# A fallback path behind a flag: its transfers move from SyncE to GpSimd, and its DMA transposes become TensorE transposes

## The chip, the cores and the metric

The kernel runs on one core of one Trainium2 chip. A core has five engines with an instruction stream each: TensorE (in the profile PE for matmuls and PEld for weight loads), VectorE (DVE), ScalarE (ACT), GpSimd (POOL) and SyncE (SP). SP does no arithmetic; it issues transfers. A "q" behind an engine's name (SPq, POOLq) means its sequencer: register, branch, semaphore and transfer-issuing instructions. The metric is device time in microseconds. The time before is 358.01 us, the median of three runs (357.88 to 358.39).

## What is computed

Causal attention with a decay that depends on the input, followed by a normalisation and a gated feed-forward layer. Batch 8, 8 heads, 576 positions, head size 64; 4608 tokens of width 512, feed-forward width 1536:

```
scores = q k^T / 8 + min(cum[j] - cum[i], 0),  cum = cumsum(max(s, 0)),  causal
x   = softmax(scores) v            # heads side by side: 4608 x 512
xn  = x / rms(x) * g
out = (silu(xn w_gate) * (xn w_val)) w_out
```

Inputs and output are float32.

## The kernel before

The program has two ways to the result. The fast path, which is nearly all of the code, folds the decay into a factor on the keys and computes exponentials without subtracting a row maximum. That holds only while scores and decay sums stay in a certain range. While it runs, it gathers what decides that: the largest absolute values of q and k (check_mag, check_max), the decay sums (decay_range) and the sums of squares. Near the end verdict() turns these into one integer, `flag_i`, on line 1063: 1 when the fast path's result stands.

The fast path walks the 4608 tokens in nine chunks of 512. For each chunk, ffn(c) (line 936) goes through 12 blocks of 128 feed-forward columns, with four matmuls for the gate (line 946) and four for the value (line 955) each, then through four blocks of 128 tokens with 12 matmuls into the output (line 972). The order of the rest is written by hand: between the matmul groups, step() puts in the attention of later tokens, by due times in slots. The whole fast path stands under one manual schedule, so its order on every engine is that of the code. At the end of each block of tokens, ACT copies the result out of PSUM (line 976) and SP stores it (line 977). The last block is stored in two parts of 384 and 128 columns. SP also issues the fast path's DMA transposes (lines 190 and 495) and some of its loads; GpSimd issues most loads.

After the fast path, general() (line 1261) is called. Line 1269 loads the flag into a register of each engine, and line 1270 opens a block that runs only when the flag is 0. When the flag is 1, each engine branches over the block:

```
flag = nc.values_load(flag_i[0:1, 0:1], min_val=0, max_val=1)
with tc.If(flag == 0, preferred_fallthrough_block=True):
```

The block computes the same result with no assumption on the range. It spills the decay sums to DRAM and has two loops. The first (line 1283) runs over the 64 pairs of batch and head: it loads q, k and v, transposes q and k on TensorE, and for each of five blocks of queries computes the scores, an ordinary softmax and the product with v; the result goes to a scratch tensor in DRAM (`x_d`). The second (line 1366) runs over the 72 groups of 64 tokens: it reads the eight heads back, normalises, transposes the 64 x 512 block, runs the feed-forward layer in three groups of 512 columns with a transpose each, and stores. Each loop ends its turn with a barrier of all engines.

Semaphores carry all order between engines. The compiler gives each transfer one of eight semaphores for those issued by SP and ACT, or one of eight for those issued by GpSimd, and each engine has its own. They count up through the program, and an instruction waits for a count. So where the block is jumped over, each engine runs a few semaphore instructions behind the branch that bring the counts to where the block would have left them; in the profile these have the line of the block, 1270. At the end of the program (line 1432, the launch), SP waits for all semaphores in twelve instructions of two each; then the engines meet in barriers and GpSimd clears the semaphores.

In the compiled program SP has 274 instructions up to its branch over the block, 186 in the block, 8 semaphore instructions for the jumped-over block, and 17 at the end.

Of the kernel before, what the change touches and what calls it, by code (L numbers as in the profile page):

```python
# [9 lines left out]
BF16 = mybir.dt.bfloat16  # L10
# [16 lines left out]
def kernel(  # L27
# [1228 lines left out]
    fast.close()  # L1256

    general(ctx, tc, q, k, v, out, wg_sb, wv_sb, wout_sb, g_row, cum, ident_bf, flag_i)


def general(ctx, tc, q, k, v, out, wg_sb, wv_sb, wout_sb, g_row, cum, ident_bf, flag_i):
    nc = tc.nc
    B, H, S, D = q.shape
    DM, FB, CC, NSC, BH = H * D, 12, 4, 5, B * H

    def rows(c):
        return 128 if c < 4 else 64

    flag = nc.values_load(flag_i[0:1, 0:1], min_val=0, max_val=1)
    with tc.If(flag == 0, preferred_fallthrough_block=True):  # L1270
        with tc.tile_pool(name="gd", bufs=1, space=bass.MemoryType.DRAM) as gd, \
             tc.tile_pool(name="gs", bufs=1) as gs, \
             tc.tile_pool(name="gp", bufs=1, space=bass.MemoryType.PSUM) as gp:
            cum_d = gd.tile([BH, S], FP32, name="cum_d")
            x_d = gd.tile([9 * BH + 56, 64, D], FP32, name="x_d")
            half = gs.tile([128, 1], FP32, name="half")
            nc.vector.memset(half, -0.5)
            nc.sync.dma_start(out=cum_d, in_=cum)
            qf = q.rearrange("b h s d -> (b h) s d")
            kf = k.rearrange("b h s d -> (b h) s d")  # L1280
            vf = v.rearrange("b h s d -> (b h) s d")
# [1 line left out]
            with tc.For_i(0, BH, 1) as i:  # L1283
                one = bass.ds(i, 1)
                nat = gs.tile([128, 2, NSC, D], BF16, name="nat")
                vn = gs.tile([128, NSC, D + 1], BF16, name="vn")
                crow = gs.tile([128, S], FP32, name="crow")
                ccol = gs.tile([128, NSC], FP32, name="ccol")
                nc.vector.memset(nat, 0.0)
                nc.vector.memset(vn, 0.0)  # L1290
                nc.vector.memset(vn[:, :, D:D + 1], 1.0)
                nc.vector.memset(ccol, 0.0)
                for w, src in ((0, kf), (1, qf)):
                    nc.gpsimd.dma_start(out=nat[:, w, 0:4, :], in_=src[one, 0:512, :].rearrange(
                        "o (c p) d -> p (o c) d", p=128))
                    nc.gpsimd.dma_start(out=nat[0:64, w, 4, :], in_=src[one, 512:576, :].rearrange(
                        "o p d -> p (o d)"))
                nc.gpsimd.dma_start(out=vn[:, 0:4, 0:D], in_=vf[one, 0:512, :].rearrange(
                    "o (c p) d -> p (o c) d", p=128))
                nc.gpsimd.dma_start(out=vn[0:64, 4, 0:D], in_=vf[one, 512:576, :].rearrange(  # L1300
                    "o p d -> p (o d)"))
                nc.sync.dma_start(out=crow, in_=cum_d[one, :].to_broadcast([128, S]))
                nc.sync.dma_start(out=ccol[:, 0:4], in_=cum_d[one, 0:512].rearrange(
                    "o (c p) -> p (o c)", p=128))
                nc.sync.dma_start(out=ccol[0:64, 4:5], in_=cum_d[one, 512:576].rearrange(
                    "o p -> p o"))
                kqt = gs.tile([D, 2, 640], BF16, name="kqt")
                for w in (0, 1):
                    pt = gp.tile([D, 640], BF16, name="pt")
                    for c in range(NSC):  # L1310
                        nc.tensor.matmul(pt[:, c * 128:(c + 1) * 128], lhsT=nat[:, w, c, :],
                                         rhs=ident_bf, is_transpose=True,
                                         start=(c == 0), stop=(c == NSC - 1))
                    nc.vector.tensor_copy(out=kqt[:, w, :], in_=pt)
                for qb in range(NSC):
                    n = rows(qb)
                    nk = qb * 128 + n
                    sp = gp.tile([128, 1024], FP32, name="sp")
                    nc.tensor.matmul(sp[0:n, 0:min(nk, 512)], lhsT=kqt[:, 1, qb * 128:qb * 128 + n],
                                     rhs=kqt[:, 0, 0:min(nk, 512)], start=True, stop=True)  # L1320
                    if nk > 512:
                        nc.tensor.matmul(sp[0:n, 512:nk], lhsT=kqt[:, 1, qb * 128:qb * 128 + n],
                                         rhs=kqt[:, 0, 512:nk], start=True, stop=True)
                    sc = gs.tile([128, 640], FP32, name="sc")
                    nc.vector.tensor_scalar(out=sc[0:n, 0:nk], in0=crow[0:n, 0:nk],
                                            scalar1=ccol[0:n, qb:qb + 1], scalar2=0.0,
                                            op0=ALU.subtract, op1=ALU.min)
                    nc.vector.scalar_tensor_tensor(out=sc[0:n, 0:nk], in0=sp[0:n, 0:nk],
                                                   scalar=0.125, in1=sc[0:n, 0:nk],
                                                   op0=ALU.mult, op1=ALU.add)  # L1330
                    nc.gpsimd.affine_select(out=sc[0:n, qb * 128:nk], in_=sc[0:n, qb * 128:nk],
                                            pattern=[[-1, n]], compare_op=ALU.is_ge,
                                            fill=-1.0e30, base=0, channel_multiplier=1)
                    mx = gs.tile([128, 1], FP32, name="mx")
                    nc.vector.tensor_reduce(out=mx[0:n], in_=sc[0:n, 0:nk], axis=AX.X, op=ALU.max,
                                            negate=True)
                    pr = gs.tile([128, 640], BF16, name="pr")
                    nc.vector.memset(pr, 0.0)
                    nc.scalar.activation(out=pr[0:n, 0:nk], in_=sc[0:n, 0:nk], func=AF.Exp,
                                         bias=mx[0:n])  # L1340
                    pq = gp.tile([128, NSC, 128], BF16, name="pq")
                    for c in range(qb + 1):
                        nc.tensor.matmul(pq[:, c, :], lhsT=pr[:, c * 128:(c + 1) * 128],
                                         rhs=ident_bf, is_transpose=True,
                                         start=(c == 0), stop=(c == qb))
                    prT = gs.tile([128, NSC, 128], BF16, name="prT")
                    nc.vector.tensor_copy(out=prT[:, 0:qb + 1, :], in_=pq[:, 0:qb + 1, :])
                    av = gp.tile([128, D + 1], FP32, name="av")
                    for c in range(qb + 1):
                        nc.tensor.matmul(av, lhsT=prT[:, c, :], rhs=vn[:, c, :],  # L1350
                                         start=(c == 0), stop=(c == qb))
                    rz = gs.tile([128, 1], FP32, name="rz")
                    nc.vector.reciprocal(out=rz[0:n], in_=av[0:n, D:D + 1])
                    xo = gs.tile([128, D], FP32, name="xo")
                    nc.vector.tensor_scalar(out=xo[0:n], in0=av[0:n, 0:D], scalar1=rz[0:n],
                                            scalar2=None, op0=ALU.mult)


                    for j in range(2 * qb, min(2 * qb + 2, 9)):
                        m = j * 64 - qb * 128  # L1360
                        nc.sync.dma_start(
                            out=x_d[bass.ds(i * 9 + 8 * j, 1)].rearrange("o p d -> p (o d)"),
                            in_=xo[m:m + 64])

            ov = out.rearrange("(t p) d -> t p d", p=64)
            with tc.For_i(0, B * 9, 1) as t:
                xb = gs.tile([64, H, D], FP32, name="xb")
                for h in range(H):
                    nc.sync.dma_start(
                        out=xb[:, h, :],  # L1370
                        in_=x_d[bass.ds(t * 8 + 9 * h, 1)].rearrange("o p d -> p (o d)"))
                sq = gs.tile([64, H, D], FP32, name="sq")
# [5 lines left out]
                xs = gs.tile([64, DM], BF16, name="xs")  # L1378
# [1 line left out]
                                               scalar=ssg, in1=g_row[0:64], op0=ALU.mult,  # L1380
                                               op1=ALU.mult)
                xT = gs.tile([128, CC, 64], BF16, name="xT")
                nc.sync.dma_start_transpose(out=xT, in_=xs)
                Hg = gs.tile([64, 3, DM], BF16, name="Hg")
                HT = gs.tile([128, 3, CC, 64], BF16, name="HT")
                for fc in range(3):
                    fs = slice(fc * DM, (fc + 1) * DM)
                    gv = gp.tile([64, 2, DM], FP32, name="gv")
                    for j, w in ((0, wg_sb), (1, wv_sb)):
                        for cc in range(CC):  # L1390
                            nc.tensor.matmul(gv[:, j, :], lhsT=xT[:, cc, :], rhs=w[:, cc, fs],
                                             start=(cc == 0), stop=(cc == CC - 1))
# [3 lines left out]
                    nc.vector.scalar_tensor_tensor(out=ug, in0=tg, scalar=1.0, in1=gv[:, 0, :],  # L1396
                                                   op0=ALU.add, op1=ALU.mult)
                    nc.vector.tensor_tensor(out=Hg[:, fc, :], in0=ug, in1=gv[:, 1, :], op=ALU.mult)
                    nc.sync.dma_start_transpose(out=HT[:, fc], in_=Hg[:, fc, :])
                og = gp.tile([64, DM], FP32, name="og")  # L1400
                for fb in range(FB):
                    nc.tensor.matmul(og, lhsT=HT[:, fb // CC, fb % CC, :], rhs=wout_sb[:, fb, :],
                                     start=(fb == 0), stop=(fb == FB - 1))
                ob = gs.tile([64, DM], FP32, name="ob")
                nc.scalar.activation(out=ob, in_=og, func=AF.Copy, scale=0.5)
                nc.sync.dma_start(out=ov[bass.ds(t, 1)].rearrange("o p d -> p (o d)"), in_=ob)


# [28 lines left out]
```

## Time and profile before

| what | value |
|---|---|
| median of three runs | 358.01 us |
| the profiled execution, in all | 358.63 us |
| its span, first to last instruction | 357.0 us |
| granted TensorE clock over the span | 0.997 |
| flag written (line 1063) | at 336.2 us |
| last matmul ends, by the chain of work | about 350.8 us |
| last instruction | 357.0 us |

The first page of the profile gives the busy time of each engine, the queues and the chain of work that ended last. Semaphore, branch and transfer-issuing instructions are not counted as busy there; they are seen by asking for one line of the kernel, which lists its instructions with count, shortest, median and longest duration in ns, and the start of the first and the last. A window limits such a list to a stretch of time, so two windows show on which side of a moment instructions lie. A row of a DMA queue gives packets, megabytes and the share of 16 engines in the window. The queues named "instruction" (q8 and q14) load the engines' code.

### The profile page before, as it was taken

How to read it: one execution, taken by the hardware profiler on the slowest of the kernel's cores; microseconds unless marked ns; L12 is line 12 of the kernel's file. 1: busy time of each engine (PE TensorE's matmuls, PEld its weight loads, DVE VectorE, ACT ScalarE, POOL GpSimd, SP SyncE). 2: the span in 40 equal slices, each digit the busy share in tenths (PEclk: the TensorE clock that was granted, in tenths of full speed). 3: DMA queues.
4: the chain of work that ended last, by engine and by line, in shares of the span. 5: the costliest groups of instructions: out<-in, count | busy, mean ns of one | idle time of the engine just before them, and what ended most of it. 6: DMA issues, size and time to landing. Idle time of an engine off the chain costs nothing.

```text
span 357.0 us, 6944 instructions
## 1 busy us (share of the span) xinstructions
PE 344.7 (97%) x2419; PEld 165.5 (46%) x2419; DVE 276.6 (77%) x524; ACT 213.4 (60%) x471; POOL 204.8 (57%) x337
## 2 busy tenths in 40 slices
PE   5989999999999999999999999999999999999993
PEld 2454444544444444544444544445444454444441
DVE  6587989598967887898889887988798579818820
ACT  3988785878786546864676467654665454223321
POOL 7968754457669977677697987597545400000000
PEclk9999999999999999999999999999999999999998
DMA  7999999999969999999899999495410221020011
GB/s 231 136 196 265 179 176 265 179 204 186 95 126 173 158 165 115 240 131 208 150 165 102 115 158 147 48 133 102 112 22 17 73 76 23 0 106 13 1 62 63
DMA packets 130528, 45.68 MB, mean 128 GB/s; under 512 B 110548, under 2 KB 125656, under 8 KB 130488
## 3 DMA queue, kind: packets, MB, share of 16 engines
q0 software_dynamic: 67056, 13.70, 49.8%
q1 hardware_dynamic: 53936, 24.26, 33.0%
q10 hardware_dynamic: 9496, 7.23, 8.2%
q8 instruction: 20, 0.33, 0.4%
q14 instruction: 20, 0.16, 0.2%
HBM read 37.90 MB, written 9.44 MB: 133 GB/s over the span
## 4 chain that ended last, share of the span: by engine, by line
PE 87%; POOL 3%; DVE 3%; issue 2%; ACT 1%; DMA 1%; SPq 0%; POOLq 0%; DVEq 0%
PE psF L972 26%; PE psF L955 23%; PE psF L946 23%; PE psS L286 2%; PE psAV L443 2%; PE psAV L437 2%; PE psF L367 2%; PE psS L367 1%; DMA kqT<-kqn 1%; POOL v_sb L409 1%; DVE x_sb L453 1%; PE psAV L1118 1%; DVE Ht L951 1%; DVE U L958 1%; PE psS L255 1%
## 5 line engine op out<-in xcount | busy, mean ns | idle before, releaser
L946 PE MATMUL psF<-xnT,wg_sb 128*128 128x512 bf16 x432 | 110.9, 379 | 0.3 <-ACT xnT L511 0.3
L955 PE MATMUL psF<-xnT,wv_sb 128*128 128x512 bf16 x432 | 111.0, 379 | 0.0
L949 ACT ACTIVATE T<-psF 128x512 f32<-128x512 f32 x108 | 64.6, 598 | 63.0 <-PE psF L946 60.9
L972 PE MATMUL psF<-wout_sb,Ht 128*128 128x512 bf16 (+2 forms) x444 | 100.9, 374 | 0.0
L958 DVE SCALAR_TENSOR_TENSOR U<-T,psF 128x512 bf16<-128x512 f32 x108 | 73.6, 682 | 24.1 <-ACT T L949 23.9
L951 DVE TENSOR_TENSOR Ht<-U,psF 128x512 bf16<-128x512 bf16 x99 | 67.8, 685 | 6.9
L972 PEld LDWEIGHTS <-Ht 128*128 128x128 bf16 x444 | 40.1, 98 | 43.5 <-issue 1.4
L955 PEld LDWEIGHTS <-wv_sb 128*128 128x128 bf16 x432 | 39.6, 98 | 44.5 <-issue 2.9
L946 PEld LDWEIGHTS <-wg_sb 128*128 128x128 bf16 x432 | 39.4, 98 | 42.9 <-issue 2.4
L976 ACT ACTIVATE osb<-psF 128x512 f32<-128x512 f32 (+2 forms) x37 | 21.7, 586 | 58.2 <-PE psF L972 51.6
L384 POOL TENSOR_SCALAR_AFFINE_SELECT E<-E 128x512 bf16<-128x512 bf16 (+1 forms) x50 | 34.8, 704 | 28.3 <-ACT E L380 18.5
L194 POOL DMA_DIRECT2D v_sb<-in_v_dram x40 | 35.2, 882 | 0.2 <-issue 0.2
L484 DVE SCALAR_TENSOR_TENSOR xs_sb<-x_sb,al_all,g_row 128x512 bf16<-128x512 bf16 (+1 forms) x36 | 29.6, 822 | 4.1 <-POOL al_all L477 3.9
L474 POOL TENSOR_SCALAR al_all<-ss_all 128x1 f32<-128x1 f32 (+2 forms) x39 | 11.5, 295 | 37.0 <-ACT xs_sb L461 29.0
L310 ACT ACTIVATE E<-psS,biasK 128x256 bf16<-128x256 f32 (+3 forms) x88 | 29.1, 425 | 2.6 <-PE psS L286 2.6
L453 DVE TENSOR_TENSOR x_sb<-psAV,rZ 128x256 bf16<-128x256 f32 (+1 forms) x66 | 28.0, 424 | 2.3
L522 DVE TENSOR_TENSOR acc<-acc,mag 128x1280 bf16<-128x1280 bf16 x32 | 27.3, 872 | 0.2
L477 POOL TENSOR_TENSOR al_all<-al_all,mhalf 128x1 f32<-128x1 f32 (+2 forms) x39 | 25.1, 645 | 3.2
L443 PEld LDWEIGHTS <-E 128*128 128x128 bf16 x320 | 21.7, 98 | 10.5 <-POOL E L384 0.7
L461 ACT ACTIVATE xs_sb<-x_sb 128x512 bf16<-128x512 bf16 (+1 forms) x37 | 23.3, 629 | 4.6 <-DVE x_sb L453 4.0
L409 POOL TENSOR_TENSOR v_sb<-v_sb,vwx 128x512 bf16<-128x512 bf16 x25 | 25.9, 1037 | 0.1
L443 PE MATMUL psAV<-v_sb,E 128*128 128x65 bf16 x264 | 23.8, 194 | 0.1
(136 smaller groups left out, 381.8 us busy)
## 6 DMA issues: line engine op xcount, KB each, us to landing
out_dram<-osb SPq DMA_DIRECT2D x35, 256.0 KB, 2.4
kq<-in_q_dram ACTq DMA_DIRECT2D x5, 1024.0 KB, 7.2
v_sb<-in_v_dram POOLq DMA_DIRECT2D x32, 128.0 KB, 5.1
kqn<-in_k_dram POOLq DMA_DIRECT2D x20, 128.0 KB, 4.8
kq<-in_k_dram SPq DMA_DIRECT2D x4, 512.0 KB, 6.0
kq<-in_q_dram SPq DMA_DIRECT2D x4, 512.0 KB, 7.6
wout_sb<-in_moe_w_out_dram POOLq DMA_DIRECT2D x2, 768.0 KB, 10.2
kq<-in_q_dram POOLq DMA_DIRECT2D x1, 1024.0 KB, 10.5
```

The source lines that it names most:

```text
L194: nc.gpsimd.dma_start(out=v_sb[0:n, b % 2, c, :, 0:64], in_=v[b, :, c * 128:c * 128 + n, :].rearrange("h p d -> p h d"))
L384: nc.gpsimd.affine_select(out=Ev, in_=Ev, pattern=[[0, 4], [1, nq]], compare_op=ALU.is_ge, fill=0.0, base=0, channel_multiplier=-1)
L409: nc.gpsimd.tensor_tensor(out=v_sb[:, b % 2, c, :, 0:64], in0=v_sb[:, b % 2, c, :, 0:64], in1=vwx[:, c, i:i + H].unsqueeze(2).to_broadcast ...
L443: nc.tensor.matmul(o, lhsT=d, rhs=v_sb[:, p, qb, h, :], start=(j == 0 and qb == 0), stop=(j == 3))
L453: nc.vector.tensor_tensor(out=xo[:, g * 256:(g + 1) * 256].rearrange("p (h d) -> p h d", h=4), in0=pv[R, :, 0:64], in1=rZ[R].unsqueeze(2). ...
L484: nc.vector.scalar_tensor_tensor(out=xs_sb[R, (b * NSC + qb) % NX, :], in0=x_sb[R, (b * NSC + qb) % NX, :], scalar=al_all[R, col:col + 1], ...
L946: nc.tensor.matmul(Gp, lhsT=wg_sb[:, cc, fs], rhs=xnT[:, cc, x0:x0 + DM], start=(cc == 0), stop=(cc == CC - 1))
L949: nc.scalar.activation(out=T, in_=Gp, func=AF.Tanh, scale=0.5)
L951: nc.vector.tensor_tensor(out=Ht[:, fb - 1, :], in0=pend[0], in1=pend[1], op=ALU.mult)
L955: nc.tensor.matmul(Vp, lhsT=wv_sb[:, cc, fs], rhs=xnT[:, cc, x0:x0 + DM], start=(cc == 0), stop=(cc == CC - 1))
L958: nc.vector.scalar_tensor_tensor(out=U, in0=T, scalar=1.0, in1=Gp, op0=ALU.add, op1=ALU.mult)
L972: nc.tensor.matmul(Op[:, p0:p1], lhsT=Ht[:, fb, tb * 128:(tb + 1) * 128], rhs=wout_sb[:, fb, p0:p1], start=(fb == 0), stop=(fb == FB - 1))
```

## The change

All edits lie in general(). Every transfer that SP issued there is issued by GpSimd: the spill of the decay sums, three loads in the first loop and its nine stores of results, the eight loads and the store of the second loop. The four DMA transposes of the second loop, which SP issued, become TensorE transposes: a helper turn() makes four 64 x 128 transposes into PSUM against the identity and copies the result to SBUF on VectorE. After the change SP issues nothing in the block. The fast path is not edited.

```
-            nc.sync.dma_start(out=cum_d, in_=cum)
+            nc.gpsimd.dma_start(out=cum_d, in_=cum)
...
-                nc.sync.dma_start(out=crow, in_=cum_d[one, :].to_broadcast([128, S]))
-                nc.sync.dma_start(out=ccol[:, 0:4], in_=cum_d[one, 0:512].rearrange(
+                nc.gpsimd.dma_start(out=crow, in_=cum_d[one, :].to_broadcast([128, S]))
+                nc.gpsimd.dma_start(out=ccol[:, 0:4], in_=cum_d[one, 0:512].rearrange(
...
-                nc.sync.dma_start(out=ccol[0:64, 4:5], in_=cum_d[one, 512:576].rearrange(
+                nc.gpsimd.dma_start(out=ccol[0:64, 4:5], in_=cum_d[one, 512:576].rearrange(
...
-                        nc.sync.dma_start(
+                        nc.gpsimd.dma_start(
                             out=x_d[bass.ds(i * 9 + 8 * j, 1)].rearrange("o p d -> p (o d)"),
                             in_=xo[m:m + 64])
+
+            def turn(dst, src):
+                px = gp.tile([128, NSC, 128], BF16, name="pq")
+                for c in range(CC):
+                    nc.tensor.matmul(px[:, c, 0:64], lhsT=src[:, c * 128:(c + 1) * 128],
+                                     rhs=ident_bf[0:64, 0:64], is_transpose=True,
+                                     start=(c == 0), stop=(c == CC - 1))
+                nc.vector.tensor_copy(out=dst, in_=px[:, 0:CC, 0:64])
...
-                    nc.sync.dma_start(
+                    nc.gpsimd.dma_start(
                         out=xb[:, h, :],
...
-                nc.sync.dma_start_transpose(out=xT, in_=xs)
+                turn(xT, xs)
...
-                    nc.sync.dma_start_transpose(out=HT[:, fc], in_=Hg[:, fc, :])
+                    turn(HT[:, fc], Hg[:, fc, :])
...
-                nc.sync.dma_start(out=ov[bass.ds(t, 1)].rearrange("o p d -> p (o d)"), in_=ob)
+                nc.gpsimd.dma_start(out=ov[bass.ds(t, 1)].rearrange("o p d -> p (o d)"), in_=ob)
```

## Prediction

> **What bounds the kernel now.** I read the first page for the engines and the chain, then the time by stretches, then the last twenty microseconds instruction by instruction, because the first two say that nothing else can move.
>
> ```profile
> span 357.0 us, 6944 instructions
> PE 344.7 (97%) x2419; PEld 165.5 (46%) x2419; DVE 276.6 (77%) x524; ACT 213.4 (60%) x471; POOL 204.8 (57%) x337
> ...
> PE 87%; POOL 3%; DVE 3%; issue 2%; ACT 1%; DMA 1%; SPq 0%; POOLq 0%; DVEq 0%
> ```
>
> TensorE is busy 97% of the span and makes 87% of the chain that ended last. That is all fast path. The line of general() that starts its block is 1270 and the launch is line 1432; here are all instructions that the trace has for line 1270 on the engines other than SP:
>
> ```profile
> L1270 POOLq COMPARE_BRANCH  x1: 45/45/45, 336.9 to 336.9; - x1
> L1270 POOLq INC_SWDGE_SEM  x1: 451/451/451, 337.8 to 337.8; - x1
> L1270 DVEq COMPARE_BRANCH  x1: 72/72/72, 341.7 to 341.7; - x1
> L1270 DVEq EVENT_SEMAPHORE  x1: 21/21/21, 342.3 to 342.3; - x1
> L1270 PEldq COMPARE_BRANCH  x1: 364/364/364, 349.6 to 349.6; - x1
> L1270 PEldq EVENT_SEMAPHORE  x1: 51/51/51, 350.9 to 350.9; - x1
> L1270 ACTq COMPARE_BRANCH  x1: 54/54/54, 351.4 to 351.4; - x1
> L1270 ACTq EVENT_SEMAPHORE  x1: 17/17/17, 351.9 to 351.9; - x1
> ```
>
> Every engine branches once, about 0.5 us later runs a few semaphore instructions, and is done. No operation of general()'s body is there: the flag says that the fast path is valid, and the block is jumped over. So no transfer, transpose or matmul of the diff is executed. What the change can alter is what an engine does because the block exists: the jump, the code that lies in between, and the semaphore instructions after the jump, which give the semaphores the counts that the block would have left (I call them catch-up). This matters only where an engine is on the path, that is, behind the last matmul, which the chain has in its last pieces (start, duration):
>
> ```profile
> 340.44 10.40 PE psF L972 x60
> 350.84 0.02 issue
> 350.86 0.28 ACT osb L976
> ```
>
> ```profile
> core 0: us, PE busy (x) PEld busy (x) DVE busy (x) ACT busy (x) POOL busy (x), PEclk, DMA share, GB/s
> 300.00:340.00 40.00, 40.00 (x187) 18.09 (x186) 27.74 (x47) 12.72 (x23) 0.00 (x0) 1.00 0.08 28
> 340.00:352.30 12.30, 10.83 (x63) 5.43 (x60) 1.38 (x2) 2.77 (x6) 0.00 (x0) 1.00 0.23 83
> 352.30:357.00 4.70, 0.00 (x0) 0.00 (x0) 0.00 (x0) 0.00 (x0) 0.00 (x0) 0.76 0.07 21
> ```
>
> From 352.3 on no engine works for 4.7 us. What runs there is SP. First its last stores, then line 1270 in two windows, then the end of the program (line 1432):
>
> ```profile
> L977 SPq DMA_DIRECT2D out_dram<-osb x2: 332/718/1103, 350.8 to 351.2; - x2
> ...
> DMA to landing us min/median/max: 2.5/2.7/2.9
> ```
>
> ```profile
> L1270 SPq EVENT_SEMAPHORE  x3: 17/17/17, 352.9 to 353.1; - x3
> L1270 SPq COMPARE_BRANCH  x1: 58/58/58, 352.3 to 352.3; - x1
> ```
>
> ```profile
> L1270 SPq EVENT_SEMAPHORE  x5: 17/17/17, 355.0 to 355.3; - x5
> ```
>
> ```profile
> L1432 SPq EVENT_SEMAPHORE  x12: 28/28/28, 355.4 to 356.1; - x12
> ```
>
> ```profile
> L1432 SPq EVENT_SEMAPHORE  x14: 17/28/28, 355.4 to 357.0; - x14
> L1432 SPq DRAIN  x3: 7/7/13, 356.1 to 356.5; - x3
> ```
>
> SP has eight catch-up instructions, one for each semaphore of its transfers; every other engine but POOL has one. Three run by 353.1, then 1.9 us pass, and the other five run from 355.0. The stores cannot explain the gap: the last is issued at 351.2 and lands at most 2.9 us later, at 354.1, and the fourth catch-up instruction belongs to an older store. The transfers in the gap are these:
>
> ```profile
> ## 3 DMA queue, kind: packets, MB, share of 16 engines
> q14 instruction: 1, 0.01, 1.8%
> q1 hardware_dynamic: 12, 0.00, 0.9%
> ```
>
> One packet that loads instructions lies between 353.1 and 354.9, beside the last dozen packets of the store. I take the gap as an instruction fetch: SP's code runs out between its third and fourth catch-up instruction. The page gives the size of such pieces:
>
> ```profile
> q8 instruction: 20, 0.33, 0.4%
> q14 instruction: 20, 0.16, 0.2%
> ```
>
> On q14 a packet is 8 KB. An instruction has 64 bytes in the compiled program, so a piece holds 128. Counted in that program (branch labels left out), SP has 274 instructions ahead of its branch, 186 more up to the first catch-up instruction, and the fourth is number 463 from zero. Two further fetches fit SP: packets in the windows 120.4 to 120.7 and 240.1 to 240.25,
>
> ```profile
> q14 instruction: 1, 0.01, 16.8%
> ```
>
> ```profile
> q14 instruction: 1, 0.01, 21.9%
> ```
>
> when SP, by its order of instructions, is just past numbers 79 and 207. Adding 128 gives 335, then 463: exactly the gap. A piece begins at 463; the one from 335 was loaded ahead at 240, so the jump itself found its target; the one from 463 was asked for only at the jump (352.4), and was there 2.6 us later.
>
> [...]
>
> **The change, part by part.**
>
> *SP's transfers inside the block (22 issues and 4 transposes in the code, 12 and 13 per turn of the two loops and one ahead).* Executed: none, cost 0. As code they are 1 + 36 + 31 instructions with their address arithmetic, plus 19 waits in the loop bodies, 16 resets and 16 catch-ups on the loops' own exits. Without them the 186 instructions shrink to about 67 (186 - 68 - 19 - 32), so the end of SP's program begins near number 340, in a piece that was loaded at 240 us. No piece begins in the 17 instructions that follow. The gap of 1.9 us goes.
>
> *The eight catch-up instructions of SP.* With no transfer of SP in the block there is nothing to catch up: eight fewer. Five of them cost 0.4 us after the gap (355.0 to 355.4), three 0.2 us before it.
>
> *What is late next.* SP now reaches the twelve paired waits of line 1432 at 352.9 instead of 355.4. They run at 0.7 us for twelve, 0.06 each. They wait for all semaphores, the last store's among them. SP would be through them at 353.6, but that store lands at 351.2 + 2.9 = 354.1. In the order of the program its pair is the eleventh, which now runs at 356.0, 1.0 before the end at 357.0. So the new end is 354.1 + 1.0 = 355.1: a gain of 1.9 us, all of it at the end. Of the 2.5 us by which SP comes earlier, 0.6 turn into a wait for the store. Bounds: with that pair first in the order, eleven more follow the landing and the end is 355.7; if the landing is as quick as the quickest of these two stores, 2.5, the end is 354.7.
>
> *POOL gets the transfers.* Executed: none. Its code grows by some 70 instructions, enough to put the jump's target outside what is loaded; bound 0 to 2.6 us (SP's fetch). It branches at 336.9 and is needed again only when SP is through, 354.1 at the earliest: 17 us of cover. Perhaps one or two more catch-ups for its semaphores, 0.1 us each, under the same cover. What it costs without cover is 2.6 us.
>
> *PE gets 16 transposes with their weight loads, DVE four copies, in code alone.* PE branches at 349.6, DVE at 341.7. If PE's longer code made its jump miss, it would come at 350.0 + 2.6 = 352.6, still ahead of 354.1. Cost 0, covered by the last store's landing. ACT's code stays as it is.
>
> *The fast path.* Its stores, transposes and loads keep their engines and order, so I count nothing.
>
> Sum against the profiled execution: 357.0 - 1.9 = 355.1 span. That execution took 358.63 in all, 0.6 above the median of 358.01 of the three runs. I carry the difference over: 358.01 - 1.9 = 356.1.
>
> **The rivals.** (a) *Half the gain.* The gap is peculiar to the profiled execution, or SP keeps its eight catch-ups after all and only the code moves. Then either the 1.9 us were not there to win, or the eighth catch-up waits for the landing (354.1) and 12 x 0.06 + 1.0 come behind it: 355.9 against 355.1. I count a gain of 0.7: 357.3. For it: one profile only. Against: the packet in the gap and the count that meets it. [...]
> (b) *The gap is a landing.* If the 355.0 were a store's landing, the same wait would reappear at the eleventh pair: end 356.0, gain 1.0, time 357.0. Against: the issue-to-landing row ends at 354.1.
> (c) *No change: the gap moves along.* My count of the shortened code is wrong and a piece that is not loaded begins at the start of the end block: SP goes on at 352.4 + 2.6 = 355.0, then twelve pairs and 1.0 to the end, 356.6: gain 0.4, time 357.6, within what can be told apart. It needs over 170 of the 186 instructions to stay.
> (d) *Slower: ACT fetches twice.* ACT is the next to last to branch (351.4, done 351.5). One fetch would end at 354.1 and cost nothing. Were its target and its end in two pieces not loaded, it would come at 356.7, SP's last pair would wait for it, and the end is 356.7 + 0.9 = 357.6, time 358.6. It decides from the point where ACT comes later than 356.1, where SP's last pair stands now. For it: ACT has little cover. Against: its code gets no instruction.
>
> **How the numbers follow.** Clean gain 70%, (a) 11%, (b) 6%, (c) 8%, (d) 5%. The three runs lie between 357.88 and 358.39, so 0.2% (0.7 us) is about what can be told from no change. Clean, (b) and half of (a) are faster: 82%; the other half and (c) are the same: 13%; slower 5%. The clean case alone gives 355.6 to 356.7 by the bounds above; the range for 8 in 10 takes in (b) and (a): 355.6 to 357.4.
>
> **What would show it.** In the changed profile: the same trace up to 352.3; on line 1270 no catch-up of SP and more on POOL near 337; the pairs of line 1432 starting near 352.9 with a wait of half a microsecond before the eleventh or so; the end near 355.1. Wrong if SP still has a gap with a fetch in it after its branch, if another engine's semaphore instruction on line 1270 or 1432 comes later than 354, if the last matmul ends elsewhere than 350.8, or if the time does not move though the gap is gone.

## The result and the profile after

The changed kernel takes 356.32 us (median of six runs, 356.02 to 357.16), against 358.39 us for the kernel before (six runs). The ratio is 0.9947, with a 95% interval of 0.9933 to 0.9961: 1.9 us less by the ratio, 2.1 us by the two medians. The profiled execution took 356.21 us, with a span of 354.7 us.

As before, nothing of general()'s body is in the trace. These are its instructions on line 1270, all engines, by the view of one line (count; shortest, median and longest duration in ns; first and last start):

```profile
L1270 POOLq EVENT_SEMAPHORE  x5: 17/43/43, 339.3 to 339.6; - x5
L1270 POOLq COMPARE_BRANCH  x1: 45/45/45, 336.6 to 336.6; - x1
...
L1270 DVEq COMPARE_BRANCH  x1: 72/72/72, 341.4 to 341.4; - x1
L1270 DVEq EVENT_SEMAPHORE  x1: 21/21/21, 342.0 to 342.0; - x1
...
L1270 PEldq EVENT_SEMAPHORE  x1: 51/51/51, 350.6 to 350.6; - x1
L1270 ACTq COMPARE_BRANCH  x1: 54/54/54, 351.1 to 351.1; - x1
L1270 ACTq EVENT_SEMAPHORE  x1: 17/17/17, 351.6 to 351.6; - x1
L1270 SPq COMPARE_BRANCH  x1: 58/58/58, 352.2 to 352.2; - x1
```

SP has its branch there and no catch-up. POOL has one semaphore instruction more than before, and its first comes 2.6 us behind its branch instead of 0.5. In the kernel before they are these, behind a branch at 336.9:

```profile
L1270 POOLq EVENT_SEMAPHORE  x4: 17/30/43, 337.4 to 337.7; - x4
```

The end of the program is now line 1440; SP's pairs there (its waits for two semaphores each), in two windows, then all of SP's instructions on that line, and what SP waited for:

```profile
L1440 SPq EVENT_SEMAPHORE  x10: 28/28/28, 352.7 to 353.3; - x10
```

```profile
L1440 SPq EVENT_SEMAPHORE  x2: 28/28/28, 353.7 to 353.7; - x2
```

```profile
L1440 SPq EVENT_SEMAPHORE  x14: 17/28/28, 352.7 to 354.6; - x14
L1440 SPq DRAIN  x3: 7/7/13, 353.8 to 354.1; - x3
```

```profile
SPq L1440 <- PEq L1440: 0.7, 2, 0.5
SPq L1440 <- DMA out_dram<-osb: 0.3, 1, 0.3
```

Ten pairs run at once from 352.7, half a microsecond behind the branch. The eleventh waits 0.3 us for the last store, and the program ends 1.0 us later. Before, the eleventh pair ran at 356.0.

The packet that the prediction saw in the gap is still there. In the changed kernel the queue q14 has from 352.4 to 354.0:

```profile
q14 instruction: 2, 0.02, 3.1%
```

The second of the two starts at 353.28, 1.1 us behind the start of SP's branch; the one in the gap before started at 353.42, also 1.1 us behind SP's branch (352.34). By this distance both are taken to be SP's. Now the pairs run on without waiting for it. So a packet in a gap does not by itself show that SP waited for the packet; the experiments below had to show that.

The chain of work ends the same way in both, a little earlier here (start, duration):

```profile
350.54 0.02 issue
350.56 0.28 ACT osb L976
```

So the span of 354.7 against 357.0 has two parts. Behind the start of the last copy (line 976) the end takes 4.15 us instead of 6.18, which is 2.0 us. The other 0.3 us lie ahead of it (350.56 against 350.86). The experiments below give no ground to put this second part down to the change: in their profiled executions the last copy starts anywhere from 349.9 to 352.5, and at 350.4 in one that leaves the block untouched. They are therefore compared by two numbers, the time from the start of that copy to the end of the span (called the tail), and the ratio of the timed runs.

### The profile page after: what moved, and what is told of

Read it like the earlier page. It is cut to its first block, busy times and chain, and to the rows that moved or that the text cites. A ratio compares the mean times of both kernels' runs of the same rounds, so it can differ in the third digit from the quotient of the medians.

```text
span 354.7 us, 6890 instructions
## 1 busy us (share of the span) xinstructions
PE 341.0 (96%) x2374; PEld 165.6 (47%) x2419; DVE 276.7 (78%) x524; ACT 213.4 (60%) x471; POOL 204.5 (58%) x337
## 4 chain that ended last, share of the span: by engine, by line
PE 78%; DVE 8%; POOL 4%; ACT 4%; issue 4%; DMA 2%; SPq 0%; POOLq 0%; DVEq 0%; ACTq 0%
PE psF L972 24%; PE psF L955 21%; PE psF L946 20%; DVE U L958 2%; PE psAV L443 2%; DMA kqT<-kqn 2%; PE psS L286 2%; DVE Ht L951 1%; PE psAV L437 1%; DVE x_sb L453 1%; PE psF L367 1%; POOL v_sb L409 1%; PE psS L367 1%; DVE xs_sb L484 1%; ACT E L326 1%
## 5 line engine op out<-in xcount | busy, mean ns | idle before, releaser
L955 PE MATMUL psF<-xnT,wv_sb 128*128 128x512 bf16 x424 | 109.9, 379 | 0.4
L946 PE MATMUL psF<-xnT,wg_sb 128*128 128x512 bf16 x414 | 109.0, 379 | 1.3 <-ACT xnT L511 0.3
L972 PE MATMUL psF<-wout_sb,Ht 128*128 128x512 bf16 (+2 forms) x428 | 98.9, 373 | 1.4 <-issue 0.8
```

What stands on the lines that cost most here:

```text
L946: nc.tensor.matmul(Gp, lhsT=wg_sb[:, cc, fs], rhs=xnT[:, cc, x0:x0 + DM], start=(cc == 0), stop=(cc == CC - 1))
L955: nc.tensor.matmul(Vp, lhsT=wv_sb[:, cc, fs], rhs=xnT[:, cc, x0:x0 + DM], start=(cc == 0), stop=(cc == CC - 1))
L972: nc.tensor.matmul(Op[:, p0:p1], lhsT=Ht[:, fb, tb * 128:(tb + 1) * 128], rhs=wout_sb[:, fb, p0:p1], start=(fb == 0), stop=(fb == FB - 1))
```

## The experiments

The theory, fetch, as read from the trace of the kernel before: SP's code is loaded in pieces of 128 instructions, one of which begins at its number 463; a piece that is not loaded at the branch is there some 2.6 us later, and SP stands until then. The main rival, landing: one of the catch-ups waits for a store. A second question is how the gain divides between the gap and the eight catch-ups.

| kernel | catch-ups of SP, by number in its code | pairs of the end begin at | tail, us | ratio to before (95%) |
|---|---|---|---|---|
| before | 460 to 467 | 468 | 6.18 | 1 |
| the change | none | 337 | 4.15 | 0.9947 (0.9933 to 0.9961) |
| loads of the second loop moved | 428 to 435 | 436 | 4.84 | 0.9952 (0.9936 to 0.9969) |
| transposes alone | 452 to 459 | 460 | 5.80 | 0.9997 (0.9981 to 1.0013) |
| transfers alone | 351 to 354 | 355 | 4.16 | 0.9928 (0.9912 to 0.9944) |
| the change and eight catch-ups | 346 to 353 | 354 | 4.92 | 0.9957 (0.9941 to 0.9972) |
| the change and 100 drains | none | 438 | 4.03 | 0.9954 (0.9940 to 0.9968) |
| the change and 120 drains | none | 458 | 5.55 | 0.9982 (0.9972 to 0.9993) |
| the change and 126 drains | none | 464 | 6.14 | 0.9980 (0.9963 to 0.9997) |
| before, last store on ScalarE | 458 to 465 | 466 | 5.15 | 0.9963 (0.9949 to 0.9976) |

The numbers in the code are counted in each compiled program, as in the prediction. A tail is that of one profiled execution. The kernel before was profiled once, the changed kernel a second time with 4.11 us. SP's issue of the last store took from 1.05 to 1.40 us in these executions, and the branch stands behind it, so differences of 0.2 us between tails say little. A ratio is to runs of the kernel before made beside it.

### Shorter code, all catch-ups kept

The kernel before, with one of the moves alone:

```
-                    nc.sync.dma_start(
+                    nc.gpsimd.dma_start(
                         out=xb[:, h, :],
```

> Only the eight loads of the second loop move from SP to GpSimd; SP keeps its other transfers, its DMA transposes and all eight catch-ups, and only its code gets shorter: the catch-ups stand at instructions 428 to 435 and the end block ends at 452, ahead of 463, where I take a new piece of code to begin. Times are counted from the end of the last matmul (before: end of the span 6.2 us behind it; after: 4.1 us). Fetch theory: no gap; the seventh catch-up waits for the last store (3.2 us behind the matmul), then the eighth and twelve pairs at 0.06 and 1.0 to the end: 5.0 us, so 1.2 us less than before (ratio 0.9966). Landing theory (a catch-up waits for a store): the gap stays where it is, 6.2 us, ratio 1.000.

SP's catch-ups, and the pairs of the end up to 353.92:

```profile
L1270 SPq EVENT_SEMAPHORE  x8: 17/17/17, 352.0 to 353.2; - x8
L1270 SPq COMPARE_BRANCH  x1: 58/58/58, 351.4 to 351.4; - x1
```

```profile
SPq L1270 <- SPq L1270: 1.2, 2, 0.7
```

```profile
L1432 SPq EVENT_SEMAPHORE  x12: 28/28/28, 353.2 to 353.9; - x12
```

All eight run within 1.2 us. The longest wait between two is 0.7 us, ahead of the seventh, which is that of the last store; the 1.9 us of before are gone. The tail is 4.84 us, 1.34 less than before (expected 1.2). The landing theory falls: SP waits for the same eight semaphores, and only where the waits stand in its code has changed.

### The transposes alone

The kernel before with turn() and its four calls, the transfers left on SP:

```
-                nc.sync.dma_start_transpose(out=xT, in_=xs)
+                turn(xT, xs)
...
-                    nc.sync.dma_start_transpose(out=HT[:, fc], in_=Hg[:, fc, :])
+                    turn(HT[:, fc], Hg[:, fc, :])
```

> Only the four DMA transposes become TensorE transposes; SP keeps its transfers and eight catch-ups. Its code gets 8 instructions shorter: catch-ups at 452 to 459, the pairs of the end from 460. Fetch theory: the eight catch-ups run without a gap (the seventh waits for the last store, 3.2 us behind the last matmul), and the gap now stands between the third and the fourth pair (462 and 463), to about 4.1 us behind the matmul; the end is at 5.6 us, 0.6 us less than before (ratio 0.9983). Landing theory: the gap stays ahead of the fourth catch-up, 6.2 us, ratio 1.000.

The catch-ups, then the pairs in two windows:

```profile
L1270 SPq EVENT_SEMAPHORE  x8: 17/17/17, 354.6 to 355.6; - x8
L1270 SPq COMPARE_BRANCH  x1: 58/58/58, 354.1 to 354.1; - x1
```

```profile
L1440 SPq EVENT_SEMAPHORE  x3: 28/28/28, 355.7 to 355.9; - x3
```

```profile
L1440 SPq EVENT_SEMAPHORE  x9: 28/28/28, 356.8 to 357.3; - x9
```

The gap has moved to just where 463 stands, between the third and the fourth pair, and ends 2.7 us behind the branch. The tail is 5.80 us, 0.4 less than before where 0.6 was expected. The ratio, 0.9997, does not show it; its interval takes in the expected 0.9983. In this profiled execution the last copy starts at 352.51, 1.65 us later than before. By the starts of the same VectorE instructions, this execution is 0.25 us ahead of the kernel before's at 160 us and 1.65 us behind it at 174 us. In between, the transposes that feed TensorE landed late (what TensorE waited for from 168 to 171.5 us):

```profile
PE psF L367 <- DMA kqT<-kqn: 1.6, 2, 0.9
```

No such wait is there in the kernel before's trace. Whether this kernel makes it likelier, or it is chance, was not settled.

### The transfers alone

All transfers of the block on GpSimd, the four DMA transposes left on SP.

> Only the transfers move to GpSimd; the four DMA transposes stay on SP, which keeps four catch-ups (none of them for the last three stores) at 351 to 354. Fetch theory: no gap, the four catch-ups cost 0.3 us that lie under the last store's landing: as the full change, end 4.1 to 4.2 us behind the last matmul, ratio 0.994 to 0.995. Landing theory: a wait as long as before shows at the eighth pair instead, end 5.4 us, ratio 0.998.

The four catch-ups cost nothing that the tail shows (4.16 us against 4.15). They run from 352.9 to 353.1, up to 2.4 us behind the start of the last copy; in the changed kernel the last store landed 3.1 us behind it. So the transfers carry the whole gain, and the transposes are not needed for it.

### The catch-ups put back, the code kept short

```
+            few = gs.tile([8, 8, 8], FP32, name="few")
+            for j in range(8):
+                nc.sync.dma_start(out=few[:, j, :], in_=cum_d[0:8, 8 * j:8 * j + 8])
```

> The changed kernel with eight small transfers of SP put back at the head of the block that is jumped over, so that SP has eight catch-ups again, but short code (catch-ups at 346 to 353). Fetch theory: no gap; the catch-ups alone cost 0.9 us, because the seventh waits for the last store and the twelve pairs now come behind it: end 5.0 us behind the last matmul, 0.9 us more than the changed kernel (ratio to before 0.997). Landing theory: the whole wait is back, 6.2 us, ratio 1.000.

```profile
L1270 SPq EVENT_SEMAPHORE  x8: 17/17/17, 352.4 to 353.6; - x8
L1270 SPq COMPARE_BRANCH  x1: 58/58/58, 351.9 to 351.9; - x1
```

The tail is 4.92 us, 0.77 more than the changed kernel. That is the price of eight catch-ups by themselves: the seventh waits for the last store, and the eighth and all twelve pairs stand behind it, where in the changed kernel ten of the pairs run ahead of it. With the 1.34 of the first experiment this makes 2.1, against 2.0 measured for the whole.

### Code that is never run, and nothing else

The changed kernel with n drains of SP at the head of the block, n = 100, 120 and 126. A drain is an instruction of which SP already has three at the end of the program; here it only stands for code:

```
+            for _ in range(120):
+                nc.sync.drain()
```

> The changed kernel with 100 drains of SP in the block that is jumped over, so code and nothing else: SP's end block stands at instructions 438 to 454 instead of 337 to 353. Fetch theory: it lies ahead of 463, in the piece that is loaded ahead, so nothing changes: end 4.1 us behind the last matmul, ratio to before 0.9947. If longer code costs by its length, or the length of a jump, some part of the 1.9 us comes back here already.

> The same with 120 drains: the end block begins at 458, so 463 is its sixth pair. Fetch theory: five pairs run at once, then a gap until 2.6 us behind the branch (4.2 us behind the last matmul), then seven pairs and the end at 5.5 us: 1.4 us more than the changed kernel, ratio to before 0.9985. Landing theory: no gap, 4.1 us, ratio 0.9947.

> The same with 126 drains: the end block begins at 464, so the branch goes to a piece that is not loaded. Fetch theory: nothing runs until 2.6 us behind the branch (4.2 us behind the last matmul), then twelve pairs and the end at 5.9 us: 1.8 us more than the changed kernel, ratio to before 0.9995 or so, though SP has no catch-up at all. Landing theory: 4.1 us, ratio 0.9947.

With 120 drains, SP's branch, then its pairs in two windows, then the instruction queue in between (353.5 to 355.2):

```profile
L1270 SPq COMPARE_BRANCH  x1: 58/58/58, 352.6 to 352.6; - x1
```

```profile
L1442 SPq EVENT_SEMAPHORE  x5: 28/28/28, 353.1 to 353.4; - x5
```

```profile
L1442 SPq EVENT_SEMAPHORE  x7: 27/28/28, 355.3 to 355.7; - x7
```

```profile
q14 instruction: 1, 0.01, 1.7%
```

With 126:

```profile
L1270 SPq COMPARE_BRANCH  x1: 58/58/58, 352.2 to 352.2; - x1
```

```profile
L1442 SPq EVENT_SEMAPHORE  x12: 28/28/28, 354.9 to 355.6; - x12
```

One hundred instructions that never run cost nothing (4.03 us). Twenty more cost 1.5 us (5.55), with the gap exactly between the fifth and the sixth pair, 462 and 463. Six more put the branch's target itself behind 463: nothing runs for 2.65 us, and the tail is 6.14 us, as long as before, without any catch-up (5.9 was expected; SP's issue of the last store took 1.40 us here, so the branch came 0.3 us later behind the copy). These kernels differ in nothing that is executed ahead of the branch, and they have no transfer of SP in the block. The gap is a fetch of code.

The times of the kernel with 126 drains do not follow its tail. Its ratio is 0.9980 where 0.9995 was expected, and the interval leaves out 1: the runs are some 0.7 us shorter than those of the kernel before, with a tail of the same length. In the profiled execution the last copy starts 0.45 us earlier (350.41). What makes the rest, and whether it is more than scatter, was not settled.

In these runs the next instruction came 0.47 us behind the branch where the target was loaded, and 2.65 us behind it with 126 drains. SP's packets have 8 KB and came, in the kernel before, at its numbers 79 and 207, 128 apart; two steps of 128 further on is 463.

### From where the time of the fetch counts

The kernel before, its block untouched, with the last store on ScalarE, so that SP branches 1.2 us earlier:

```
-                nc.sync.dma_start(out=out[r0:r0 + 128, p0:p1], in_=osb[:, p0:p1])
+                eng = nc.scalar if p0 else nc.sync
+                eng.dma_start(out=out[r0:r0 + 128, p0:p1], in_=osb[:, p0:p1])
```

> The kernel before, its general path untouched, with the last store (128 columns) issued by ScalarE. SP branches as soon as its store of the 384 columns is issued, about 0.3 us behind the last matmul instead of 1.5. Its code ahead of the branch is two instructions shorter, so 463 is now its sixth catch-up. Fetch theory: five catch-ups, then a gap until 2.6 us behind the branch, 2.9 us behind the last matmul; three catch-ups, twelve pairs and the end at 4.9 us instead of 6.2: ratio 0.9963, though nothing of the block's code goes and all eight catch-ups stay. If the gap were of fixed length behind a store's landing (2.8 us here, 3.1 before), the end would move by 0.3 us at most, ratio 0.999.

```profile
L1271 SPq EVENT_SEMAPHORE  x5: 17/17/17, 351.2 to 351.6; - x5
```

```profile
L1271 SPq EVENT_SEMAPHORE  x3: 17/17/17, 353.7 to 353.9; - x3
```

Five catch-ups, the gap, three catch-ups, as counted. The gap ends 2.9 us behind the branch, 0.3 more than elsewhere, and the tail is 5.15 us (expected 4.9), the ratio 0.9963 as expected.

The sixth catch-up happens to be the one that waits for SP's store of the 384 columns. SP issued that store at 350.3, and the landings of the last two stores took:

```profile
DMA to landing us min/median/max: 2.7/2.8/2.9
```

The longest is that store's, so it landed at 353.3, and the gap ended 0.4 us later, at 353.7. Where a landing did end a wait, at the changed kernel's eleventh pair, the semaphore instruction ran 0.02 us behind it (353.667 and 353.684). So this landing is not taken to have ended the gap.

The packet of q14 that is taken for SP's by its distance from the branch starts at 351.88, 1.2 us behind SP's branch, where it was 1.1 us in the kernel before and in the changed kernel. It takes 0.1 us longer than before, and SP goes on 0.1 us later behind its end, which with the later start makes the 0.3 us. So the time of the fetch counts from the branch: SP branches 1.2 us sooner behind the last copy, and the gap ends 0.9 us sooner, though the last store lands only 0.2 us sooner.

### The same store moved in the changed kernel

> The changed kernel, with the last store (128 columns) issued by ScalarE behind its own copy instead of by SP. In the changed kernel SP's issue of it takes 1.26 us, against 0.33 for the others, because it comes 0.4 us behind the store of the 384 columns, and its landing ends the wait of the eleventh pair. If the issue is what is late: landing about 2.6 us behind the last matmul instead of 3.1, end 3.6 to 3.8 us instead of 4.1, ratio to before 0.9935 to 0.9940. If the landing is bound by the two stores' packets: no change, ratio 0.9947; and if ScalarE's own branch becomes late, its own semaphore instruction would stand beyond 3 us.

> The changed kernel with the last store issued by ScalarE once more: end 3.8 us behind the last matmul, 0.3 us ahead of the changed kernel, ratio lower than the changed kernel's by 0.001.

> The changed kernel as it is, in the same call as the next, so that the two share the runs of the kernel before: end 4.1 us behind the last matmul, ratio 0.994 to 0.996.

This is the changed kernel with the edit just shown, in two sets of runs, and the changed kernel itself beside the second. ScalarE issues the store in 0.38 us where SP took 1.26. It lands 2.8 and 3.0 us behind the start of the last copy, against 3.1 for the changed kernel, so sooner, but not by as much as expected (2.6). The tail is 3.81 and 4.00 us in the two profiled executions, against 4.15 and 4.11. The times do not separate them: 0.9927 (0.9913 to 0.9941) in the first set, and in the second 0.9928 (0.9914 to 0.9942) beside 0.9932 (0.9918 to 0.9946) for the changed kernel. Both tails are shorter, by 0.1 to 0.3 us, which is near what tails differ by anyway; a gain in the time is not shown.

## The prediction, point by point

**Nothing of the block is run: right.** Apart from line 1270 the traces have nothing of it.

**The gap is a fetch of code, at number 463: right,** and shown by moving it three ways: ahead of the boundary (gone), across it (at the pair that was counted), and behind it (the whole end waits). The 64 bytes of an instruction, which the prediction has from the compiled program, agree with the trace: 8 KB to a packet, over the 128 numbers between the two fetches.

**The gap of 1.9 us and the eight catch-ups go, and a wait for the last store is left: right.** The prediction had the 1.9 us of gain as one number, ended by the store's landing, and did not divide it. Taken apart, the gap is worth 1.34 us while the catch-ups stay, and the catch-ups 0.77 once the gap is gone. Together they are worth 2.0 in the changed kernel.

**The code shrinks by 119 instructions to about 67, and the end begins near 340: right** (67, counted with the branch as in the prediction, and 337). Four register moves at the head of SP's program went too, which the prediction did not count; they only shift all of SP's numbers by four.

**What is late next is the last store: right.** The wait is 0.3 us where 0.6 were expected, because SP's issue of that store took 1.26 us in this execution against 1.10 before, so SP branched later by as much, and the store landed 0.08 us sooner behind the last copy. The end comes 1.0 us behind the pair, as read from the profile before.

**POOL's longer code costs up to 2.6 us under 17 us of cover: right.** Its first catch-up stands at 339.3, 2.6 us behind its branch at 336.6, where it was 0.5. It is next needed at 353.9. The prediction's list of line 1270, which it calls all of the other engines, lacks POOL's four semaphore instructions (337.4 to 337.7); nothing rests on them.

**PE, DVE and ACT cost nothing: right.** DVE and ACT have their semaphore instruction 0.6 and 0.5 us behind the start of their branch (342.0 and 351.6), as before, and PE has its own at 350.6, where the last matmul ends (350.54).

**The sum: 356.1 predicted, 356.32 measured.** The 1.9 us of gain that were forecast are what the ratio gives, and the tail gives 2.0. The start of 358.01 was the median of three runs; the six beside the changed kernel have 358.39, so the closeness of the two times owes something to chance, and that of the gains less. The span came out at 354.7 where 355.1 was predicted. The 0.4 us are 0.3 from ahead of the last copy, which varies between executions, and 0.1 from the tail.

**The rivals.** (a), half the gain, was wrong as a cause: the gap is no accident of one profiled execution, since it stood or was gone in every one as the count of instructions said, and SP has no catch-ups left. The 0.8 us that it put on kept catch-ups (355.9 against 355.1) is near the 0.77 measured; the one that waits for the store is the seventh, not the eighth. (b), a landing, fell with the first experiment. (c), the gap moving along, did not happen in the change. A boundary just at the end block is the kernel with 126 drains: the tail there is 6.14 us, as long as before, where (c) counted a gain of 0.4. (d) did not happen: ACT's semaphore instruction stands at 351.6, half a microsecond behind its branch.

## What to carry to other kernels

The block that is jumped over cost 2.0 us here, at the end, on the engine that finishes last: its semaphores had to be caught up (0.77 us once the gap was gone), and its code lay between the branch and the rest of the program (1.34 us while the catch-ups stayed). So try giving rare work to an engine that is done early, as POOL was here with 17 us to spare, and read the stretch behind the last matmul instruction by instruction: in these profiles no engine counts as busy once the last copy is done, and the chain of work ends with that copy. And before a difference of half a per cent is put down to an edit, ask where it moves the code: here 20 instructions that never ran made 1.5 us.

## What the runs showed of the hardware that was not expected

On SP a branch to code that, by the count, was loaded cost 0.47 us from its end to the next instruction in every kernel here. To code that was not, it cost 2.65 us (126 drains). Where the code ran out later, SP went on 2.60, 2.61, 2.69 and 2.91 us behind the branch (before, 120 drains, transposes alone, before with the last store on ScalarE). POOL's 2.6 us in the changed kernel look like the same; that was not tried by padding its code. The packet in SP's gap, and the two at its numbers 79 and 207, have 8 KB each. On q8, the queue of 16 KB packets, nothing was tried; by the 64 bytes that 8 KB over 128 numbers make, its 20 packets would hold 5120 instructions, which is near the 4885 that the trace of the kernel before has of TensorE. This is an estimate from the counts alone.

The second of two stores issued by SP 0.4 us apart held SP for 1.0 to 1.4 us in all kernels that have it; on ScalarE the same store took 0.38 us to issue. Why SP is held was not looked into; that it is the 0.4 us, as an expectation above has it, no run shows.

The fast path, which is the same in all kernels up to the last store, put the last copy between 349.9 and 352.5 us. By the starts of the same VectorE instructions, differences of up to 1.1 us against the kernel before stand there 20 us into the span; one of 1.9 us arose where TensorE waited for a DMA transpose. They go into the time ratios and not into the tails.
